# A newly searched order of steps, PSUM banks and engines in a fused attention and FFN kernel

## The chip, the cores and the metric

The kernel runs on one core of a Trainium2 chip. The metric is the device time of one execution in microseconds. The core has five engines with a queue of instructions each: TensorE (PE in the profile, its weight loads PEld), VectorE (DVE), ScalarE (ACT), GpSimd (POOL) and SyncE (SP). GpSimd and SyncE do hardly any arithmetic here: they issue the DMA transfers, ScalarE a few.

## What is computed

Linear attention with exponential features, and behind it a feed-forward network (FFN) with a squared ReLU. B is 8, H 8, S 576, D 64, the features 128, the model width 512, the FFN width 2048.

```
def phi(x):
    proj = np.einsum('bhsd,df->bhsf', x, w_phi)
    proj = proj - np.max(np.abs(proj), axis=-1, keepdims=True)
    return np.concatenate([np.exp(proj), np.exp(-proj)], axis=-1)
q_p, k_p = (phi(q), phi(k))
kv = np.einsum('bhsf,bhsd->bhfd', k_p, v)
z = np.sum(k_p, axis=2)
num = np.einsum('bhsf,bhfd->bhsd', q_p, kv)
den = np.einsum('bhsf,bhf->bhs', q_p, z)[..., None] + 1e-06
...
h = np.maximum(x @ w_in, 0.0)
return (h * h @ w_out).astype(np.float32)
```

Between the two, the 8 batches of attention output are laid out as 4608 tokens of width 512.

## The kernel before, in words

**Steps.** The kernel first lists 1680 steps in a plan, each with its engine, what it reads and writes, and a number in the order of listing (`add`, `Plan`). A step is one instruction, or a short run of matmuls, or one DMA. Then `plan.arrange()` gives the steps in the order of the list `ORDER`, and the last loop issues them so. `pin` ties each instruction to the one before on its engine, so every engine works through its own steps strictly in the order in which `ORDER` names them; SyncE's and GpSimd's DMA issues are such steps too. Across engines only the data and the buffers bind. Four more lists belong to `ORDER`:

- `BASES` gives each of the 377 uses of PSUM its bank.
- `STATES` says, for steps that two engines can do (copies out of PSUM, the ReLU of the FFN, the cast of the first k), which one does.
- `GATES` names for each load of batches 2 to 7 one step that it waits for beside its data, so that it isn't issued early.
- `FILL` puts n matmuls of zeros on TensorE ahead of a step, into a bank that is free there (line 961). They compute nothing that is used.

**Attention** of a batch works in groups of heads: Pk and Pq (L347, L379, L491) project k and q by `w_phi` in matmuls on half of the array's rows (64), two beside one another; Mk and Mq (L386, L405, L498, L531) take the maxima on VectorE; Ekp, Ekn, Eqp, Eqn (L394, L411, L544, L584) the exponentials on ScalarE; V (L428) scales v; KVs and KV (L450 on 64 rows, L462) sum up kv; the copy of kv to SBUF is kvc. For the output NA (L599, L648) multiplies the positive features, SA (L610, L660) scales the sum in PSUM, NB adds the negative ones, rd and xo (L614 to L674) divide. For batches 0 and 1 k and q are turned by TensorE (Txk, Txq, L320, with copies Cxk, Cxq on VectorE or ScalarE), and batch 0's output too (Tx, Txh, copies Cx, Cxh, L631, L699). Fq (L569) makes q's features already turned. From batch 2 on, k and q are turned by DMA transposes that SyncE issues (Xxk, Xxq, L331), the output of batches 1 to 7 by Xx (L708), and the features of q in batches 3 to 7 by Xf (L548). Xf reads one of two buffers qf, so the exponentials for the next but one group wait until it has landed.

**FFN.** Nine chunks of 512 tokens: one for each batch, and one of the 64 last tokens of every batch. F1 (L788; for chunk 0 in smaller pieces f1a, f1b, f1, f1p at L813, L799, L827) multiplies by `w_in`, relu and sq (L765, L767, L774) follow on ScalarE and VectorE, F2 (L882, the last tile F2h at L846) by `w_out`; ot copies the result, st stores it. Attention of batch c + 1 and the FFN of chunk c are mixed in `ORDER`.

**The beginning, by number.** 0 and 1: the first part of k by ScalarE's queue, cast by kcast:7 and 8. 2: `w_phi` by SyncE, cast by wcast:3 and 4. 6 and 5: VectorE sets the zeros of the fillers and of the identity matrix; ident:11 on GpSimd (L913) makes the identity of it, which every Txk needs. 9, 10: the 64 last tokens of batch 0's k; 12, 13: the rest of its k; 14, 19: its q; 15 to 18: its v; 26: batch 1's k, 1 MB of f32 that lands as 512 KB of bf16; 22 to 25: `w_in`; 36 to 39: `w_out`. All these loads are issued by GpSimd. 40, 49, 58, 66, 74 turn the five groups of k of batch 0, 42, 51, 60, 68, 76 project them.

Of the kernel before, what the change touches and what calls it, by code (L numbers as in the profile page):

```python
# [108 lines left out]
def kernel(  # L109
# [869 lines left out]
    210, 342, 242, 346, 243, 205, 485, 336, 224, 236, 233, 347, 267, 276, 226, 268, 182, 352, 183, 227, 277, 364,  # L979
    337, 353, 269, 366, 192, 489, 193, 549, 235, 278, 373, 254, 338, 237, 238, 490, 255, 239, 247, 257, 258, 241,  # L980
    228, 248, 259, 240, 229, 249, 230, 260, 270, 374, 333, 285, 232, 231, 343, 271, 244, 261, 272, 286, 262, 495,
    273, 274, 263, 344, 499, 287, 264, 265, 503, 339, 266, 294, 251, 295, 507, 252, 275, 296, 279, 250, 508, 288,
    280, 513, 253, 551, 289, 281, 547, 349, 282, 283, 556, 290, 354, 350, 284, 375, 379, 553, 291, 256, 292, 517,
    377, 744, 381, 348, 293, 297, 345, 531, 367, 376, 382, 298, 535, 370, 378, 380, 369, 299, 521, 552, 351, 422,
    300, 548, 387, 423, 525, 390, 546, 539, 557, 526, 389, 301, 371, 543, 388, 554, 413, 544, 438, 550, 482, 439,
    414, 372, 486, 440, 563, 483, 429, 368, 487, 416, 430, 383, 747, 492, 384, 555, 431, 474, 484, 740, 564, 395,
    417, 385, 478, 500, 475, 386, 476, 504, 479, 501, 488, 391, 480, 505, 514, 392, 493, 302, 510, 494, 393, 506,
    496, 511, 527, 404, 405, 565, 502, 396, 532, 497, 394, 498, 522, 398, 515, 518, 406, 523, 516, 540, 491, 519,
    397, 545, 533, 419, 524, 754, 447, 420, 399, 541, 400, 559, 448, 401, 749, 407, 408, 582, 403, 402, 449, 741,
    409, 583, 536, 739, 424, 415, 432, 562, 584, 410, 433, 737, 528, 411, 512, 418, 561, 520, 412, 434, 421, 529,  # L990
# [12 lines left out]
    627, 648, 780, 776, 1128, 913, 649, 929, 797, 650, 917, 651, 775, 899, 796, 921, 811, 774, 798, 903, 787, 781,
    831, 659, 782, 799, 783, 925, 784, 785, 786, 660, 860, 926, 832, 661, 873, 861, 864, 946, 662, 833, 663, 878,
    788, 834, 868, 862, 865, 907, 869, 664, 870, 819, 879, 886, 822, 880, 896, 866, 821, 856, 897, 887, 823, 820,
    882, 857, 812, 800, 874, 1312, 883, 789, 908, 942, 858, 801, 900, 884, 927, 875, 1120, 891, 876, 904, 901, 941,
    888, 902, 948, 1119, 790, 905, 949, 791, 1122, 792, 802, 951, 892, 898, 950, 793, 803, 824, 906, 893, 914, 835,
    794, 804, 894, 805, 843, 915, 825, 922, 845, 826, 916, 813, 923, 827, 806, 814, 918, 844, 815, 919, 910, 816,
    817, 846, 1068, 847, 828, 911, 829, 986, 924, 964, 960, 967, 1050, 830, 836, 1072, 848, 965, 962, 1321, 909,
    1124, 1054, 818, 849, 920, 966, 1123, 961, 1058, 1129, 988, 837, 912, 944, 1076, 838, 977, 963, 1121, 987, 1080,  # L1010
    1132, 839, 1081, 1062, 940, 840, 841, 978, 989, 1104, 1063, 842, 956, 998, 952, 1001, 990, 1086, 953, 1090, 1000,
    957, 1094, 955, 1002, 979, 1108, 954, 999, 1098, 968, 959, 970, 850, 1051, 969, 851, 1137, 958, 1059, 980, 1099,
    1112, 1052, 1060, 971, 852, 1126, 1047, 853, 1130, 854, 1010, 1116, 1127, 1013, 855, 1134, 1055, 1048, 1011, 991,
    1125, 1117, 1065, 1003, 1136, 1049, 1015, 1012, 1061, 1077, 1056, 1073, 1014, 1057, 1078, 1066, 1022, 1074, 1053,
# [93 lines left out]
```

## Time and profile before

| what | value |
|---|---|
| median of 3 runs | 347.04 us (346.59 to 347.21) |
| the profiled execution's own time | 346.94 us |
| its span, from first to last instruction | 345.2 us |
| granted TensorE clock, mean | 1.000 |
| moved by DMA | 51.51 MB, mean 149 GB/s |

The profile is of one execution. Busy times of an engine are sums over its instructions; matmuls overlap, so their durations are longer than their spacing from start to start. "Idle before" names what ended an idle time. The chain that ended last is followed back from the last instruction. Rows of the timeline give start, duration, engine, line, operation and tiles, with a count where equal instructions in a row are merged. A few matmul records can be missing, so a count of 15 can stand for 16.

### The profile page before, as it was taken

How to read it: one execution, taken by the hardware profiler on the slowest of the kernel's cores; microseconds unless marked ns; L12 is line 12 of the kernel's file. 1: busy time of each engine (PE TensorE's matmuls, PEld its weight loads, DVE VectorE, ACT ScalarE, POOL GpSimd, SP SyncE). 2: the span in 40 equal slices, each digit the busy share in tenths (PEclk: the TensorE clock that was granted, in tenths of full speed). 3: DMA queues.
4: the chain of work that ended last, by engine and by line, in shares of the span. 5: the costliest groups of instructions: out<-in, count | busy, mean ns of one | idle time of the engine just before them, and what ended most of it. 6: DMA issues, size and time to landing. Idle time of an engine off the chain costs nothing.

```text
span 345.2 us, 8387 instructions
## 1 busy us (share of the span) xinstructions
PE 333.0 (96%) x3361; PEld 188.2 (55%) x3393; DVE 262.7 (76%) x477; ACT 228.5 (66%) x401; POOL 95.5 (28%) x143
## 2 busy tenths in 40 slices
PE   7899999999999999999999999989999999999995
PEld 6679866545554554545545655545555454444443
DVE  2999998999887898799888888967888735655230
ACT  4998897588897996677887888497476213241121
POOL 8662550971910570104604160430000000000000
PEclk9999999999999999999999999999999999999999
DMA  9999999999999999999999999999882831100206
GB/s 129 169 190 194 197 178 176 124 142 247 124 170 197 207 156 197 190 186 191 186 186 169 201 187 180 169 133 154 182 166 54 170 92 56 45 0 2 91 32 151
DMA packets 142935, 51.51 MB, mean 149 GB/s; under 512 B 111472, under 2 KB 138416, under 8 KB 142896
## 3 DMA queue, kind: packets, MB, share of 16 engines
q1 hardware_dynamic: 97488, 32.35, 49.8%
q0 software_dynamic: 44960, 18.23, 47.5%
q8 instruction: 26, 0.43, 0.5%
q10 hardware_dynamic: 448, 0.39, 0.4%
q14 instruction: 13, 0.11, 0.1%
HBM read 36.73 MB, written 9.44 MB: 134 GB/s over the span
## 4 chain that ended last, share of the span: by engine, by line
PE 83%; DMA 6%; DVE 4%; ACT 2%; POOL 2%; issue 1%; SPq 1%; POOLq 0%; DVEq 0%; ACTq 0%
PE psum L882 32%; PE psum L788 30%; PE psum L648 5%; PE psum L347 5%; PE psum L462 3%; DMA xv<-in_v_dram 2%; PE psum L827 2%; DMA qpn<-qf 2%; DMA xT<-xo 1%; DVE mq L498 1%; PE psum L799 1%; PE psum L813 1%; PE psum L846 1%; PE psum L569 1%; DVE va L428 1%
## 5 line engine op out<-in xcount | busy, mean ns | idle before, releaser
L882 PE MATMUL psum<-wout,h 128*128 128x512 bf16 x528 | 128.2, 379 | 2.1 <-issue 0.6
L788 PE MATMUL psum<-xT,win 128*128 128x512 bf16 x448 | 105.5, 379 | 1.9 <-ACT hr L765 1.1
L765 ACT ACTIVATE hr<-psum 128x512 bf16<-128x512 f32 x103 | 60.2, 603 | 57.0 <-PE psum L788 35.3
L882 PEld LDWEIGHTS <-h 128*128 128x128 bf16 x560 | 51.4, 98 | 56.3
L788 PEld LDWEIGHTS <-win 128*128 128x128 bf16 x512 | 46.9, 98 | 53.5 <-issue 1.6
L774 DVE TENSOR_TENSOR h<-hr 128x512 bf16<-128x512 bf16 x144 | 56.4, 417 | 10.1 <-ACT hr L765 9.4
L544 ACT ACTIVATE qf<-psum 128x1024 bf16<-128x1024 f32 (+1 forms) x50 | 45.5, 942 | 15.1 <-PE psum L347 10.1
L405 DVE TENSOR_REDUCE mk<-psum 128x8 f32<-128x1024 f32 (+1 forms) x38 | 42.3, 1121 | 6.9 <-ACT kn L411 2.0
L767 DVE TENSOR_SCALAR hr<-psum 128x512 bf16<-128x512 f32 x41 | 27.8, 686 | 17.9 <-PE psum L788 17.3
L411 ACT ACTIVATE kn<-psum 128x1024 bf16<-128x1024 f32 (+1 forms) x38 | 35.7, 947 | 6.4 <-PE psum L347 4.7
L411 ACT ACTIVATE kp<-psum 128x1024 bf16<-128x1024 f32 (+1 forms) x38 | 35.5, 950 | 4.5 <-PE psum L347 3.0
L660 DVE TENSOR_TENSOR psum<-psum,en 128x520 f32<-128x520 f32 (+1 forms) x39 | 27.0, 701 | 13.5 <-ACT en L514 7.4
L648 PEld LDWEIGHTS <-qpn 128*128 128x128 bf16 x624 | 27.5, 98 | 13.4 <-issue 0.6
L269 POOL DMA_DIRECT2D xq<-in_q_dram x24 | 17.3, 725 | 52.2 <-DVE mq L531 14.2
L648 PE MATMUL psum<-kv,qpn 128*128 128x65 bf16 x624 | 30.6, 193 | 0.0
L531 DVE TENSOR_REDUCE mq<-psum 128x8 f32<-128x1024 f32 (+1 forms) x25 | 27.8, 1111 | 2.8 <-ACT qf L544 1.7
L584 ACT ACTIVATE qpn<-psum 128x1024 bf16<-128x1024 f32 (+1 forms) x30 | 26.8, 955 | 2.2 <-PE psum L569 1.3
L674 DVE TENSOR_TENSOR xo<-psum,rden 128x512 bf16<-128x512 f32 (+1 forms) x39 | 26.5, 686 | 0.8
L249 POOL DMA_DIRECT2D xk<-in_k_dram x27 | 19.8, 738 | 21.9 <-ACT en L508 14.6
L195 ACT ACTIVATE ot<-psum 128x512 f32<-128x512 f32 x23 | 13.8, 600 | 16.2 <-PE psum L882 16.1
L249 POOL DMA_DIRECT2D xv<-in_v_dram x27 | 19.9, 747 | 15.7 <-PE psum L648 11.1
L428 DVE TENSOR_TENSOR va<-xv,va 128x1280 bf16<-128x1280 bf16 (+2 forms) x34 | 23.5, 714 | 0.1
(78 smaller groups left out, 349.4 us busy)
## 6 DMA issues: line engine op xcount, KB each, us to landing
out_dram<-ot SPq DMA_DIRECT2D x32, 256.0 KB, 2.9
xk<-in_k_dram POOLq DMA_DIRECT2D x25, 128.0 KB, 5.4
xq<-in_q_dram POOLq DMA_DIRECT2D x24, 128.0 KB, 5.1
xv<-in_v_dram POOLq DMA_DIRECT2D x24, 128.0 KB, 5.0
win<-in_moe_w_in_dram POOLq DMA_DIRECT2D x4, 512.0 KB, 8.8
wout<-in_moe_w_out_dram POOLq DMA_DIRECT2D x4, 512.0 KB, 12.9
xq<-in_q_dram POOLq DMA_DIRECT2D x4, 256.0 KB, 7.2
out_dram<-ot SPq DMA_DIRECT2D x6, 128.0 KB, 2.4
```

The lines of the kernel that those rows point to most:

```text
L249: pin(nc.gpsimd.dma_start(out=x[:, m0 + a * 512 : m0 + z * 512].rearrange("p (h x) -> p h x", x=4 * D), in_=src[b][2 * a : 2 * z, 0:512, : ...
L405: pin(nc.vector.tensor_reduce(out=mk_view(g), in_=ps2(pj)[:, :, : n * Fd].rearrange("p e (i f) -> p e i f", f=Fd), axis=AX.X, op=ALU.max, ...
L411: pin(nc.scalar.activation(out=dst[slot][:, :, :n, :].rearrange("p e i f -> p e (i f)"), in_=ps2(pj)[:, :, : n * Fd], func=ACT.Exp, scale= ...
L531: pin(nc.vector.tensor_reduce(out=mqb[:, c, :, :n], in_=ps2(pj)[:, :, : n * Fd].rearrange("p e (i f) -> p e i f", f=Fd), axis=AX.X, op=ALU ...
L544: pin(nc.scalar.activation(out=o, in_=i_, func=ACT.Exp, scale=sgn))
L648: pin(nc.tensor.matmul(out=o[:, u // 4, u % 4 * D1 : (u % 4 + 1) * D1], lhsT=qpn[slot][:, sg * half + u * m : sg * half + u * m + P], rhs= ...
L660: pin(nc.vector.tensor_tensor(out=o, in0=o, in1=enb[:m, c, :].rearrange("t (b h) -> t b h", b=2).to_broadcast([m, 2, 4, D1]), op=ALU.mult))
L765: pin(nc.scalar.activation(out=hr[sl], in_=ps1(g), func=ACT.Relu))
L767: pin(nc.vector.tensor_scalar(out=hr[sl], in0=ps1(g), scalar1=0.0, scalar2=None, op0=ALU.max))
L774: pin(nc.vector.tensor_tensor(out=dst, in0=i_, in1=i_, op=ALU.mult))
L788: pin(nc.tensor.matmul(out=o, lhsT=win[mc // 4][:, kc, mc % 4 * P : (mc % 4 + 1) * P], rhs=x, start=(kc == 0), stop=(kc == KC - 1)))
L882: pin(nc.tensor.matmul(out=ps1(g), lhsT=h2[c % 2][mc // 4][:, mc % 4, tt * P : (tt + 1) * P], rhs=wout[mc // 4][:, mc % 4, :], start=(mc = ...
```

## The change

The plan, the steps and the code that issues them stay. The five lists are replaced: `ORDER` is another order of the same 1680 numbers, with the DMA issues at other places in it as well; `BASES`, `STATES` (82 steps instead of 80 on their other engine) and `GATES` are others; `FILL` has 117 matmuls before 12 steps instead of 119 before 11. On VectorE step 5 (the zeros of the identity) comes behind kcast:7 and wcast:3, and kcast:7 and 8 are VectorE's instead of ScalarE's. On GpSimd the first steps are 13, 9, 19, 11, 12, 14, 10, 26, 18, 17, 15 where they were 13, 12, 11, 14, 10, 9, 19, 18, 17, 16, 15, 26. The chunk 0 FFN starts with f1a:311 instead of f1a:307.

The diff, cut to the first lines of `ORDER`, the stretches in which the steps 464, 1181 and 1229 stand, and `FILL`:

```
 ORDER = [
-    2, 0, 1, 13, 12, 7, 8, 6, 5, 11, 3, 14, 10, 40, 41, 9, 4, 42, 19, 46, 74, 66, 44, 18, 43, 58, 45, 17, 75, 67, 47,
-    76, 16, 59, 68, 79, 48, 15, 71, 90, 77, 26, 88, 60, 21, 70, 91, 89, 28, 78, 49, 69, 27, 50, 20, 94, 80, 61, 81,
-    51, 72, 73, 92, 30, 95, 93, 98, 57, 22, 62, 52, 99, 31, 64, 54, 55, 23, 85, 53, 56, 84, 131, 24, 63, 82, 156, 25,
-    132, 157, 101, 37, 65, 133, 212, 83, 29, 128, 86, 102, 109, 87, 32, 110, 213, 111, 103, 129, 194, 214, 130, 104,
-    113, 215, 105, 112, 195, 96, 106, 100, 97, 365, 188, 107, 108, 218, 36, 217, 189, 114, 219, 121, 134, 34, 115,
-    216, 122, 116, 206, 33, 135, 123, 200, 207, 124, 38, 159, 117, 125, 201, 118, 136, 126, 160, 190, 137, 127, 119,
-    191, 142, 120, 161, 138, 145, 143, 220, 146, 307, 139, 308, 360, 147, 140, 221, 311, 312, 309, 162, 158, 141,
-    303, 144, 313, 163, 148, 223, 304, 149, 164, 322, 305, 165, 310, 166, 150, 323, 319, 151, 306, 234, 222, 152,
-    315, 314, 316, 320, 196, 325, 198, 321, 317, 197, 167, 153, 326, 328, 168, 154, 199, 318, 155, 169, 170, 174,
-    329, 324, 208, 356, 171, 186, 175, 331, 35, 209, 187, 176, 39, 245, 332, 184, 246, 177, 361, 172, 185, 334, 173,
-    359, 211, 178, 202, 357, 340, 203, 335, 355, 179, 477, 330, 358, 204, 180, 327, 481, 181, 363, 341, 225, 362,
...
-    745, 569, 708, 460, 428, 573, 712, 455, 587, 586, 461, 616, 462, 468, 463, 619, 690, 509, 469, 464, 609, 618,
-    578, 470, 716, 471, 580, 620, 472, 694, 617, 717, 581, 698, 628, 579, 736, 640, 631, 695, 756, 699, 665, 629,
...
-    1161, 1253, 1162, 1168, 1290, 1250, 1194, 1214, 1153, 1328, 1238, 1041, 1239, 1242, 1042, 1251, 1264, 1243, 1181,
-    1169, 1244, 1043, 1246, 1252, 1044, 1254, 1260, 1247, 1240, 1045, 1216, 1268, 1317, 1170, 1255, 1046, 1295, 1215,
-    1323, 1269, 1248, 1322, 1299, 1261, 1265, 1326, 1163, 1270, 1201, 1330, 1319, 1202, 1256, 1332, 1164, 1331, 1204,
...
-    1229, 1198, 1490, 1222, 1210, 1223, 1494, 1199, 1291, 1211, 1498, 1224, 1346, 1499, 1368, 1380, 1371, 1200, 1458,
-    1381, 1468, 1370, 1446, 1347, 1212, 1472, 1382, 1369, 1476, 1383, 1480, 1353, 1350, 1384, 1352, 1462, 1481, 1349,
...
-    40: (0, 26), 42: (0, 12), 76: (3, 11), 90: (1, 11), 49: (5, 2), 94: (5, 10), 98: (3, 4), 131: (7, 28),
-    212: (7, 6), 214: (7, 6), 116: (7, 3),
+    2, 0, 1, 13, 9, 19, 6, 7, 3, 5, 11, 8, 12, 4, 40, 14, 41, 42, 47, 10, 48, 74, 66, 75, 26, 44, 67, 76, 43, 45, 18,
+    68, 71, 77, 17, 58, 15, 46, 94, 69, 79, 27, 21, 59, 81, 70, 95, 49, 16, 60, 50, 78, 61, 51, 28, 90, 20, 73, 55,
+    88, 91, 72, 53, 30, 89, 92, 56, 57, 63, 98, 93, 24, 52, 54, 99, 156, 65, 34, 62, 206, 212, 22, 157, 131, 207,
+    101, 23, 64, 132, 218, 213, 25, 128, 82, 133, 31, 83, 102, 29, 129, 104, 105, 80, 103, 32, 106, 84, 194, 35, 85,
+    214, 100, 219, 86, 109, 110, 361, 87, 108, 215, 195, 111, 130, 33, 107, 200, 112, 96, 114, 36, 113, 201, 216,
+    115, 121, 134, 37, 122, 188, 116, 135, 97, 123, 217, 38, 190, 124, 117, 136, 125, 137, 39, 158, 118, 189, 142,
+    138, 159, 191, 143, 145, 160, 366, 126, 119, 127, 146, 220, 120, 139, 311, 140, 161, 312, 141, 221, 303, 144,
+    313, 148, 304, 147, 149, 307, 305, 308, 222, 150, 196, 151, 322, 152, 309, 233, 306, 199, 162, 310, 319, 163,
+    323, 197, 223, 164, 315, 165, 316, 166, 320, 153, 314, 317, 170, 154, 167, 171, 198, 186, 325, 187, 168, 155,
+    173, 169, 324, 208, 326, 174, 318, 331, 321, 175, 327, 172, 176, 209, 328, 332, 177, 329, 245, 178, 184, 210,
+    340, 185, 330, 179, 211, 546, 334, 180, 181, 356, 341, 202, 246, 337, 205, 357, 477, 342, 335, 203, 358, 338,
...
+    569, 558, 686, 572, 567, 461, 455, 616, 462, 712, 463, 619, 571, 464, 468, 690, 618, 469, 694, 573, 620, 617,
+    470, 716, 471, 472, 578, 717, 628, 579, 698, 586, 473, 609, 928, 630, 665, 588, 699, 755, 587, 669, 631, 666,
...
+    1152, 1160, 1149, 1299, 1159, 1150, 1118, 1161, 1250, 1181, 1254, 1215, 1242, 1162, 1251, 1041, 1238, 1182, 1042,
+    1216, 1252, 1260, 1239, 1243, 1043, 1246, 1318, 1044, 1244, 1045, 1133, 1261, 1303, 1240, 1169, 1247, 1134, 1201,
+    1248, 1330, 1322, 1264, 1332, 1262, 1202, 1168, 1320, 1333, 1268, 1325, 1331, 1204, 1256, 1269, 1307, 1218, 1203,
...
+    1486, 1351, 1228, 1337, 1195, 1490, 1196, 1226, 1440, 1302, 1207, 1219, 1208, 1197, 1444, 1229, 1220, 1209, 1198,
+    1445, 1494, 1210, 1211, 1327, 1221, 1498, 1212, 1222, 1199, 1468, 1223, 1499, 1200, 1230, 1368, 1380, 1346, 1383,
...
+    40: (0, 26), 42: (0, 11), 74: (3, 5), 76: (3, 7), 58: (4, 10), 49: (1, 24), 51: (5, 1), 88: (2, 4), 92: (2, 3),
+    156: (2, 6), 104: (5, 17), 121: (6, 3),
```

More of the change, by code (lines that the diff above doesn't have):

```diff
@@ L967 @@
 ORDER = [
[81 rows of a table removed]
[81 rows of a table added]
 ]
 BASES = (
[L1051 to L1054 removed]
+    '2014344022667555460560154672607205225563225457457070405242534266666056300064674474775442572340044070'
+    '5464242600246660633232227661207363176020027654260622044644756455643420345250220426732466426444401111'
+    '1002301311203026246413452664604002001133112370020710166224247652046500226664050652107151674773052075'
+    '37206240040034273250265436735646454673234753512671743126027144306542632647167'
 )
 STATES = (
[L1057 to L1059 removed]
+    '0000000000010000011111010110011000000000000100001000101110000100000010000111011001000100000001000111'
+    '0101011100100000001000000110000000011010010110100010001000101000011100000000011011000000101110101100'
+    '011001110100110110101000110011101'
 )
 GATES = {
[11 rows of a table removed]
[11 rows of a table added]
 }
 FILL = {
[L1075 to L1076 removed]
+    40: (0, 26), 42: (0, 11), 74: (3, 5), 76: (3, 7), 58: (4, 10), 49: (1, 24), 51: (5, 1), 88: (2, 4), 92: (2, 3),
+    156: (2, 6), 104: (5, 17), 121: (6, 3),
 }
```

7 lines of the change are left out of this document (removed), and 148 rows, old and new, of tables (GATES, ORDER).

## Prediction

> **What bounds the kernel now.** I read the page, then busy time by stretches, then who waited for whom on TensorE.
>
> ```profile
> span 345.2 us, 8387 instructions
> PE 333.0 (96%) x3361; PEld 188.2 (55%) x3393; DVE 262.7 (76%) x477; ACT 228.5 (66%) x401; POOL 95.5 (28%) x143
> PE 83%; DMA 6%; DVE 4%; ACT 2%; POOL 2%; issue 1%; SPq 1%; POOLq 0%; DVEq 0%; ACTq 0%
> ```
> ```profile
> 0.00:10.00 10.00, 7.55 (x106) 6.55 (x107) 3.64 (x11) 5.29 (x9) 8.89 (x17) 1.00 1.14 133
> 10.00:20.00 10.00, 8.29 (x122) 6.15 (x120) 10.00 (x16) 10.00 (x21) 5.44 (x9) 1.00 1.49 177
> 20.00:30.00 10.00, 9.76 (x198) 8.12 (x197) 9.24 (x21) 9.53 (x18) 6.25 (x9) 1.00 1.24 194
> ```
> ```profile
> PE psum L788 <- ACT hr L765: 1.1, 1, 1.1
> PE psum L788 <- DMA xT<-xo: 0.8, 1, 0.8
> ```
>
> TensorE is busy 96% of the span and carries 83% of the chain that ended last. The columns of the stretches are length, then PE, PEld, DVE, ACT, POOL busy, clock, DMA share, GB/s. In the second and third stretch VectorE (10.00, 9.24) and ScalarE (10.00, 9.53) are full while TensorE still has holes, which the filler matmuls partly paint over. So there are two regimes: a head that VectorE, ScalarE and the loads set, and a long body that TensorE sets. The chain shows where they meet:
>
> ```profile
> 8.11 8.09 DMA xv<-in_v_dram
> 28.46 0.55 PE psum L813 x8
> 337.98 3.51 PE psum L846 x32
> ```
>
> The first FFN matmuls start at 28.46, the last end at 341.49: 313.0 us in which TensorE waited for others only 1.1 + 0.8 us by the wait rows above. The rest is the same matmuls in any order, so a new order can win only these 1.9 us, the cost of changing between kinds of matmul, and some of the head.
>
> **The body: changes of array form.**
>
> ```profile
> 207.19 1.02 PE L882 MATMUL psum<-wout,h 128*128 128x512 bf16 x4
> 208.15 0.62 PE L347 MATMUL psum<-wphi,kT 64*128 64x128 bf16 x16
> 208.61 0.39 PE L347 MATMUL psum<-wphi,qT 64*128 64x128 bf16 x8
> 208.93 3.63 PE L882 MATMUL psum<-wout,h 128*128 128x512 bf16 x15
> 212.39 1.89 PE L788 MATMUL psum<-xT,win 128*128 128x512 bf16 x8
> 214.12 0.41 PE L648 MATMUL psum<-kv,qpn 128*128 128x65 bf16 x8
> ```
>
> Eight L788 matmuls take 214.12 - 212.39 = 1.73 us, 0.216 each, and an eight-fold L648 follows free of charge. Four L882 ought to take 0.86, but the 64-row L347 starts 0.96 later: 0.10 to go in. Sixteen L347 take 0.46, so eight take 0.23, and L882 starts 0.32 after them: 0.09 to come out. A visit to the 64-row form (Pk, Pq, Fq, KVs) costs about 0.2 us. Counting such visits in the two ORDER lists from the first f1a on gives 47 before and 45 after: **-0.4 us** (bounds 0 and -0.6, as the price differs by neighbour). Tx:139, four transposes of 0.056, now stands before the first f1a: **-0.2** of body.
>
> **The head.**
>
> ```profile
> 0.90 0.11 DVE L238 MEMSET ident<- 128x64 uint32 x1
> 2.90 0.32 POOL L913 TENSOR_SCALAR_AFFINE_SELECT ident<-ident 128x128 bf16<-128x128 bf16 x1
> 4.27 0.81 ACT L195 ACTIVATE xk<-ot 128x256 bf16<-128x256 f32 x2 [1.33 <-DMA ot<-in_k_dram]
> 4.44 0.31 DVE L230 CAST wphi<-wphi_f 64x128 bf16<-64x128 f32 x1 [3.43 <-DMA wphi_f<-in_w_phi_dram]
> 4.74 0.68 PE L320 MATMUL psum<-ident,xk 128*128 128x128 bf16 x4 [0.79 <-ACT xk L195]
> ```
>
> Now step 5, the memset of ident at 0.90, stands on VectorE behind kcast:7 and wcast:3, which wait for loads until 4.27 and 4.44. So it runs near 4.8, and POOL's ident:11, at 2.90 before, near 5.0. POOL issues in order: ident:11 comes after three loads (13, 9, 19), which end near 3.7, and **xk:12, xq:14, xks:10, xk:26 and all of V stand behind it**, some 1.3 us of POOL standing still. Txk:40 starts near 5.4 instead of 4.74, so VectorE's stream starts about 0.35 later. The next price is VectorE's work up to Cxh:120, which releases the first f1a:
>
> ```profile
> 5.46 0.42 DVE L193 COPY kT<-psum 128x512 bf16<-128x512 bf16 x1 [0.71 <-PE psum L320]
> 7.35 0.69 DVE L386 TENSOR_REDUCE mk<-psum 128x4 f32<-128x512 f32 x1 [1.10 <-ACT kp L394]
> 23.50 0.42 DVE L193 COPY qT<-psum 128x512 bf16<-128x512 bf16 x1
> 23.83 0.41 DVE L193 COPY kT<-psum 128x512 bf16<-128x512 bf16 x1
> 27.13 0.28 DVE L631 COPY xT<-psum 128x256 bf16<-128x256 bf16 x1
> 27.32 0.68 DVE L674 TENSOR_TENSOR xo<-psum,rden 128x512 bf16<-128x512 f32 x1
> 27.92 1.21 DVE L498 TENSOR_REDUCE mq<-psum 128x8 f32<-128x1024 f32 x1
> ```
>
> From 5.46 to 27.41 is 21.95 us, of which 1.9 wait (1.10 at 7.35). Put ahead of Cxh:120 are four copies (Cxq:95, 93, Cxk:50, 201) of 23.83 - 23.50 = 0.33, xo:138 (0.60) and Mq:143 (1.21): 3.13. Gone from there are three copies (Cxq:189, 191, Cxk:219), kvc:108 and a wcast (0.35 each): 1.69. Net +1.44. The wait at 7.35 goes, as Mk:48 now stands ahead of the exponentials of its bank; new waits come at Cxk:50 (xks:10 is late) and at V. With waits of 0.7 to 1.9, Cxh:120 ends at 5.8 + 20.05 + 1.44 + (0.7 to 1.9) = 28.0 to 29.2 and f1a starts 0.2 later. Before, f1a was held until 28.46 by other TensorE work. I take 28.9: **+0.45** (bounds -0.2 and +0.95).
>
> Loads could make it worse:
>
> ```profile
> xk<-in_k_dram POOLq DMA_DIRECT2D x1, 512.0 KB, 10.0
> 18.89 0.40 PE L320 MATMUL psum<-ident,xk 128*128 128x128 bf16 x4 [0.46 <-DMA xk<-in_k_dram]
> ```
>
> xk:26 landed at about 18.8, 2.6 after V at 16.20: the loads of this queue land in order of issue. Now it is issued ahead of V, with two small loads more, so V lands near 18 and 19.5. VectorE reaches the first V near 17.4 (2.2 us of other work was put ahead), so about 0.6 of this shows, and is in the waits above. The Trainium skill, "DMA: Bandwidth & Descriptors", section "Anatomy of one DMA", fits a transfer of this path at 2.0 us plus its bytes at 436 GB/s; by that 512 KB lands in 3.2 us, no load would bind, and the head would be an estimated 0.7 us better. The row's 10.0 speaks against it for a full queue.
>
> ```profile
> 26.16 3.87 ACT L584 ACTIVATE qpn<-psum 128x1024 bf16<-128x1024 f32 x4
> ```
>
> ScalarE: these four exponentials (Eqp:160 to Eqn:147) now stand behind Cxq:189 and 191 and start about 1.2 later, with a relu between them, ending near 32.1; NB:150 would run at 31.8. **+0.3** (bounds 0 and +1).
>
> **The body's waits.** SP issues in order, and a transpose blocks it for long.
>
> ```profile
> 98.05 3.32 SPq L331 DMA_TRANSPOSE kT<-xk  x1
> 106.14 4.40 DMA xT<-xo
> 214.12 2.77 SPq L331
> 216.94 7.26 DMA qpn<-qf
> 224.28 1.02 ACT L544 ACTIVATE qf<-psum 128x1024 bf16<-128x1024 f32 x1 [2.27 <-DMA qpn<-qf]
> DMA to landing us min/median/max: 3.1/5.2/8.6
> ```
>
> The 0.8 wait: Xx:464 issued at 106.14, late behind Xxk:755 (3.32) and others, and landed after 4.40, with three F2 groups (2.6) and 1.3 of small work standing between it and its first F1. After, four F2 groups (3.45) and 1.15 stand there, and Xxk:755 comes behind it: **-0.8** (bounds 0 and -0.9). The 1.1 wait: Xf:1181, behind Xxk:1328 (2.77), took 7.26; ScalarE stood 2.27 at Eqn:1204, with the relu that TensorE wanted behind it. Both transposes keep their order, and the TensorE work between Xf:1181 and Eqn:1204 grows only from 6.6 to 7.1: **0** (bounds -1.1 and +0.5). New risk: between Xf:1229 and Eqn:1383 stand 3.8 us (6.1 before, to its first user then), and before Xf:823's first user 5.9 (8.5), against landings of 3.1 to 8.6: **+0.2** (bounds 0 and +2). PSUM banks and the 82 instead of 80 steps on their other engine cost nothing by themselves: VectorE is 76% busy over the span. The tail keeps its last 32 F2h matmuls and stores. Fillers are 117 instead of 119, in holes.
>
> **Sum:** -0.4 - 0.2 + 0.45 + 0.3 - 0.8 + 0 + 0.2 = -0.45 us. The profiled execution took 346.94 (span 345.2 and 1.7 around it), 0.1 under the median 347.04. So 346.5 in the profiled run's terms and **346.6** beside the median.
>
> **Rivals.**
> 1. *No waits:* both old waits vanish, none forms, NB:150 isn't held. -0.4 - 0.2 + 0.45 - 1.9 = -2.05: 345.0. For: most distances from Xx to F1 are longer. Against: the Xf pattern at 1181 is unchanged. 0.12.
> 2. *Waits form elsewhere* behind transposes: at Eqn:1383 1.1 and at one F1 0.8 instead of 0.2: +1.25, 348.3. For: landings up to 8.6 against 3.8 and 5.9. Against: later on ScalarE has slack. 0.17.
> 3. *Slower by the head:* POOL's pause behind ident:11 leaves the load queue dry, and V lands 1.3 us later than I reckon, near 19.4; the first V on VectorE then waits 2 us instead of 0.6. It decides once V's first half lands after about 18. Price +1.4 to +1.6: +1.05, 348.1. For: V's landing is on the chain (8.09). Against: three loads are queued before the pause. 0.22.
> 4. *The head isn't bound by loads:* VectorE then waits only 0.7, f1a starts at 28.2, -0.25 instead of +0.45: -1.15, 345.9. For: 2.2 us of other work stand ahead of V. Against: the 10.0 us of the load ahead of V. 0.04. The Trainium skill's fit, named above, would come to this.
> 5. *The lists change nothing that matters:* the engines keep to ORDER, but every shift is absorbed: 347.0. 0.03.
>
> **Numbers.** The forecast, 345.6 to 347.2, has 0.42, of it 0.24 below 346.35 and 0.18 above. A measurement of this kernel tells about 0.2% (0.7 us) from no change. Faster: 0.24 + 0.12 + 0.04 = 0.40. Same: 0.18 + 0.03 = 0.21. Slower: 0.17 + 0.22 = 0.39. The range takes in rivals 2 to 5 and the upper half of rival 1: 344.9 to 348.9.
>
> **What would show it.** The ident memset near 4.8 and the affine select near 5.0 on POOL; the first L813 matmul at 28.6 to 29.2 (over 30: rival 3); no TensorE wait for xT near 110; a ScalarE wait for qpn<-qf near 223 followed by a TensorE wait for hr. Between the first L813 and the last L846 I expect 312.1 us; under 311 is rival 1, over 313.5 rival 2. If ident's memset runs before 2 us, or V holds VectorE for none or over 1.5 us, the head is wrong; if waits of TensorE above 0.5 us appear at other places than these, the body is.

## The result, and the profile after

| | kernel before | changed kernel |
|---|---|---|
| median of 4 executions | 346.81 us (346.58 to 347.21) | 353.39 us (351.32 to 357.63) |
| the profiled execution's own time | 346.94 us | 357.63 us |
| its mean granted TensorE clock | 1.000 | 0.985 |
| first L813 (start of the body) | 28.46 us | 29.23 us |
| last L846 (end of the body) | 341.49 us | 352.17 us |

The changed kernel is slower: ratio 1.0159 (95% interval 1.0119 to 1.0200). I had put the range at 344.9 to 348.9 us and slower by over 0.2% at 0.39; the time lies 4.5 us above the range. All ratios here leave out executions more than 1.5% above their kernel's fastest, which also hits some whose own waits are merely longer, so medians over all executions stand beside them.

The page of the changed kernel, the lines that answer to those of the kernel before, with the row of the granted clock, which was all nines there:

```profile
span 355.9 us, 8414 instructions
PE 337.5 (95%) x3361; PEld 190.0 (53%) x3391; DVE 266.5 (75%) x485; ACT 224.5 (63%) x393; POOL 95.6 (27%) x143
PEclk9998999999999999989989999999999999999999
PE 80%; DMA 8%; DVE 4%; ACT 4%; issue 2%; POOL 1%; SPq 0%; DVEq 0%; ACTq 0%
```

DMA has 8% of the chain instead of 6%, and in three slices the clock falls to eight tenths. Who waited for whom, TensorE's rows (us in total, times, longest):

```profile
PE psum L788 <- ACT qf L544: 4.0, 1, 4.0
...
PE psum L347 <- DVE xo L674: 2.7, 1, 2.7
...
PE psum L882 <- DVE ot L193: 0.8, 1, 0.8
...
PE psum L462 <- DVE va L428: 0.4, 1, 0.4
```

Both old waits (0.8 for xT, 1.1 for hr) are gone and two long new ones have come; with two small ones they are 7.9 us in the body instead of 1.9. The chain, from three windows of it, shows what stands behind each:

```profile
29.23 2.26 PE psum L813 x24
```
```profile
144.88 10.04 DMA qpn<-qf
...
155.00 0.16 ACT qf L544
...
157.10 4.44 PE psum L788 x12
```
```profile
175.31 7.72 DMA xT<-xo
...
183.12 0.70 DVE xo L674
...
183.87 0.40 PE psum L347 x8
184.26 2.71 PE psum L882 x7
```

Near 157: the transpose Xf:799, issued at 144.88, takes 10.04 us. ScalarE stands at Eqp:821, which overwrites the buffer qf that Xf:799 reads; behind it, in ScalarE's order, is the exponential that frees the bank of the next F1. Near 184: Xx:806, issued at 175.31, takes 7.72 us. VectorE stands at xo:841, which overwrites the xo that Xx:806 reads, and a Pk waits for its banks. In both a transpose gives a buffer back late, and an engine that works in order carries the wait to TensorE.

Look also at the matmuls right after: twelve L788 take 4.44 us, 0.37 each instead of 0.216. The table by stretches (length, then busy time of PE, PEld, DVE, ACT, POOL, then the clock) shows why:

```profile
24.20:27.62 3.42, 2.48 (x28) 1.34 (x29) 2.43 (x8) 2.47 (x5) 1.45 (x2) 1.00 1.24 206
27.62:31.03 3.41, 3.31 (x35) 2.94 (x34) 2.42 (x6) 2.40 (x5) 0.91 (x2) 0.50 1.44 195
...
153.90:157.32 3.42, 0.22 (x2) 0.10 (x2) 1.03 (x2) 2.32 (x6) 0.00 (x0) 1.00 1.08 148
157.32:160.73 3.41, 3.41 (x10) 1.17 (x9) 0.90 (x2) 2.21 (x4) 0.00 (x0) 0.50 1.29 270
...
181.20:184.63 3.43, 0.77 (x10) 0.43 (x10) 1.51 (x3) 1.10 (x2) 0.00 (x0) 1.00 1.31 59
184.63:188.04 3.41, 3.19 (x8) 1.21 (x8) 3.41 (x4) 2.86 (x4) 0.00 (x0) 0.50 0.79 143
```

Three times a stretch in which TensorE had stood idle for a part (it was busy 2.48, 0.22 and 0.77 us of some 3.42) is followed by 3.41 us at clock 0.50, which cost 1.7 us each. With that the account of the profiled execution, the longest of the four, closes: the body starts 0.8 later, has 6.0 us more of waits, and loses 1.8 + 3.4 + 3.4 us at half clock, which is 4.3 us; that makes 11.1, the measured difference is 10.7, and the remaining -0.4 is the body's own work. Set apart: 311.2 us of body without waits before, 310.8 after. The new order costs nothing where nothing waits; it loses by late transposes and by the half clock behind them.

### The profile page after: what moved, and what is told of

Same layout as the page of the kernel before. It is cut to its first block, busy times and chain, and to the rows that moved or that the text cites. A ratio compares the mean times of both kernels' runs of the same rounds, so it can differ in the third digit from the quotient of the medians.

```text
span 355.9 us, 8414 instructions
## 1 busy us (share of the span) xinstructions
PE 337.5 (95%) x3361; PEld 190.0 (53%) x3391; DVE 266.5 (75%) x485; ACT 224.5 (63%) x393; POOL 95.6 (27%) x143
## 4 chain that ended last, share of the span: by engine, by line
PE 80%; DMA 8%; DVE 4%; ACT 4%; issue 2%; POOL 1%; SPq 0%; DVEq 0%; ACTq 0%
PE psum L882 32%; PE psum L788 27%; PE psum L648 5%; PE psum L347 5%; PE psum L462 4%; DMA qpn<-qf 3%; DMA xT<-xo 2%; PE psum L827 2%; DMA xv<-in_v_dram 2%; PE psum L813 1%; ACT qpn L584 1%; PE psum L799 1%; DVE mq L498 1%; PE psum L846 1%; DVE mk L405 1%
## 5 line engine op out<-in xcount | busy, mean ns | idle before, releaser
L882 PE MATMUL psum<-wout,h 128*128 128x512 bf16 x530 | 129.4, 382 | 2.9 <-issue 0.9
L788 PE MATMUL psum<-xT,win 128*128 128x512 bf16 x448 | 107.4, 383 | 4.0 <-ACT qf L544 4.0
L765 ACT ACTIVATE hr<-psum 128x512 bf16<-128x512 f32 x96 | 56.2, 599 | 56.2 <-PE psum L788 28.4
L882 PEld LDWEIGHTS <-h 128*128 128x128 bf16 x560 | 51.7, 98 | 57.9 <-issue 3.4
L788 PEld LDWEIGHTS <-win 128*128 128x128 bf16 x512 | 47.4, 98 | 56.3 <-issue 6.5
L405 DVE TENSOR_REDUCE mk<-psum 128x8 f32<-128x1024 f32 (+1 forms) x38 | 42.3, 1119 | 3.8 <-PE psum L347 2.5
L767 DVE TENSOR_SCALAR hr<-psum 128x512 bf16<-128x512 f32 x48 | 32.7, 686 | 11.4 <-PE psum L788 9.4
L249 POOL DMA_DIRECT2D xk<-in_k_dram x27 | 19.7, 733 | 68.7 <-PE psum L788 11.6
L195 ACT ACTIVATE ot<-psum 128x512 f32<-128x512 f32 x19 | 11.3, 597 | 33.2 <-PE psum L882 33.2
L193 DVE COPY ot<-psum 128x512 f32<-128x512 f32 x16 | 11.0, 688 | 26.4 <-PE psum L882 25.7
L531 DVE TENSOR_REDUCE mq<-psum 128x8 f32<-128x1024 f32 (+1 forms) x25 | 27.6, 1109 | 1.7 <-PE psum L347 1.1
## 6 DMA issues: line engine op xcount, KB each, us to landing
wout<-in_moe_w_out_dram POOLq DMA_DIRECT2D x4, 512.0 KB, 11.1
```

The costliest lines, as they stand in the source:

```text
L249: pin(nc.gpsimd.dma_start(out=x[:, m0 + a * 512 : m0 + z * 512].rearrange("p (h x) -> p h x", x=4 * D), in_=src[b][2 * a : 2 * z, 0:512, : ...
L405: pin(nc.vector.tensor_reduce(out=mk_view(g), in_=ps2(pj)[:, :, : n * Fd].rearrange("p e (i f) -> p e i f", f=Fd), axis=AX.X, op=ALU.max, ...
L531: pin(nc.vector.tensor_reduce(out=mqb[:, c, :, :n], in_=ps2(pj)[:, :, : n * Fd].rearrange("p e (i f) -> p e i f", f=Fd), axis=AX.X, op=ALU ...
L765: pin(nc.scalar.activation(out=hr[sl], in_=ps1(g), func=ACT.Relu))
L767: pin(nc.vector.tensor_scalar(out=hr[sl], in0=ps1(g), scalar1=0.0, scalar2=None, op0=ALU.max))
L788: pin(nc.tensor.matmul(out=o, lhsT=win[mc // 4][:, kc, mc % 4 * P : (mc % 4 + 1) * P], rhs=x, start=(kc == 0), stop=(kc == KC - 1)))
```

## The experiments

**Theory A:** the loads of the next batches share the DMA engines with the transposes; the new lists put a burst of fourteen loads (129 to 143 us) beside them, so these land late. **Theory B:** the new order of the three compute engines leaves the transposes too little room, whatever the queues do. **Theory C:** SyncE's new order issues them too late. In what part loads and transposes would hinder one another (the engines, the memory) no run here separates.

**1. The changed kernel again**

> The changed kernel once more, unaltered, to see which of its losses come back. The profile shown has two long waits of TensorE (4.0 us behind ScalarE's wait for qpn<-qf near 157, 2.7 us behind VectorE's wait for xT<-xo near 184), and three stretches of 3.41 us at half clock, each of which costs 1.71 us. If the waits belong to the order, both are in this profile again, over 2 us each, and the times lie in steps of about 1.7 us between 350 and 358. If they are chance of one execution, they are gone or elsewhere, and the times are near 350.

Median 354.05 us over 6 executions (350.04 to 358.30), ratio 1.0119 [1.0075, 1.0163]. Its profile is of an execution of 351.53 us without half clock:

```profile
ACT qf L544 <- DMA qpn<-qf: 9.8, 3, 4.4
...
DVE xo L674 <- DMA xT<-xo: 2.0, 1, 2.0
...
PE psum L788 <- ACT qf L544: 1.8, 1, 1.8
...
PE psum L347 <- DVE xo L674: 1.6, 1, 1.6
...
PE psum L882 <- ACT hr L765: 1.5, 1, 1.5
```

The same two waits at the same steps, but shorter than the 2 us each that were expected, a third of 1.5 behind Xf:823 (the user that the prediction gave 5.9 us of room) and smaller ones, 7.3 us in all; so their places belong to the order, and their length to the execution. Less what their mean clocks (0.984 to 1.000) say was lost, the times lie between 348.7 and 352.6. The first L813 is at 27.72 here: the body started 0.7 us earlier than in the kernel before, which contradicts the prediction's head.

**2. The loads later.** Nine loads of the burst are moved behind Mq:832 and wait for it.

```
-    933: 454, 934: 467, 935: 653, 936: 589, 937: 872, 938: 474, 939: 592,
+    933: 454, 934: 832, 935: 832, 936: 832, 937: 832, 938: 832, 939: 832,
...
-    943: 619,
+    943: 832,
...
-    1126: 881, 1129: 417,
+    1126: 832, 1129: 832,
```

> Nine of the fourteen loads that GpSimd issues between 129 and 143 us are held until Mq:832 (about 150). Theory that the loads crowd out the transposes: Xx:627 to Xf:799 land after 4 to 6.5 us instead of 8.7 to 10.0, ScalarE waits under 1 us for qpn<-qf at Eqp:821, the 4.0 us wait of TensorE near 157 falls under 0.8, and the half-clock stretch behind it goes too: 4 to 5.5 us off a run that has both. Rival, that the transposes are slow since SyncE issues them in a bunch: their landings stay over 8 us and the wait stays over 3 us. The wait near 184 stays in both.

Median 358.20 us (355.71 to 364.28), ratio 1.0295 [1.0253, 1.0337]: 4 us worse. But Xf:811 and Xf:799 now landed after 4.4 and 5.3 us, and the wait near 157 is gone, as theory A said. What came instead shows in SyncE's issues:

```profile
148.03 0.90 SPq L900 DMA_DIRECT2D out_dram<-ot  x1
159.79 4.52 SPq L331 DMA_TRANSPOSE qT<-xq  x1
164.41 1.79 SPq L548 DMA_TRANSPOSE qpn<-qf  x1
```

SyncE stood from 149 to 159.8 at Xxq:947, which needs the loads that I held back, and Xf:823, ready at 150.2, stood behind it; TensorE waited 10.0 us in one piece near 170. A wait moved from one in-order queue into another is not removed.

**3. Xx:806 first.** SyncE's steps, taken out of `ORDER`:

```
-    835, 909, 847, 818, 806, 830,
+    835, 806, 909, 847, 818, 830,
```

> In SyncE's order Xx:806 stands right behind Xf:835, as in the kernel before, and no longer behind st:909, Xf:847 and Xx:818. Theory that SyncE's order makes the second wait: Xx:806 is issued 3.4 us earlier (near 171.9 instead of 175.3), lands near 179, VectorE no longer waits for it at xo:841, the 2.7 us wait of TensorE near 184 falls under 0.5, and its half-clock stretch goes: 2.5 to 4.4 us. Rival, that the loads between 172.7 and 178 make it land late: it still lands after 182 and at least 2 us of the wait stay. The wait near 157 stays in both.

```profile
166.16 4.06 SPq L548 DMA_TRANSPOSE qpn<-qf  x1
170.31 1.22 SPq L708 DMA_TRANSPOSE xT<-xo  x1
```

Issued at 170.31 instead of 175.31, Xx:806 landed after 3.8 us instead of 7.72; xo:841 ran at 178.23 without waiting, and the wait near 184 is gone from the profile (the one near 157 was 3.9 there). Median 351.56 us over 12 executions (347.36 to 353.69), ratio 1.0078 [1.0035, 1.0121]: 2.5 us below the 354.05 of the unaltered kernel in the same rounds, though the intervals of the two ratios overlap. So at this place theory C holds: SyncE's order put the transpose where it was late. Theory A has a share in it: in the unaltered kernel Xx:806 stood among nine loads issued from 172.72 to 178.06, here it went ahead of them all.

**4. Fillers in the two waits**

```
-    156: (2, 6), 104: (5, 17), 121: (6, 3),
+    156: (2, 6), 104: (5, 17), 121: (6, 3), 882: (1, 50), 952: (6, 32),
```

> 50 filler matmuls (2.8 us) are put before the F1 that waits near 157 and 32 (1.8 us) before the Pk that waits near 184; nothing else. Theory that the half clock is the price of an idle TensorE and comes on top of the wait: where the two waits are long, the F1 and the Pk start at the same time as without fillers, but no half-clock stretch follows them, so a run that had both is 3.4 us shorter, and the mean clock is 0.995 or more in every run. Rival, that the clock falls for another reason: half-clock stretches remain behind both places and the times stay as in the unaltered kernel.

```profile
152.92 2.95 PE L961 MATMUL psum<-warm 128*128 128x128 bf16 x50 [0.25 <-DVE hr L767]
156.28 1.89 PE L788 MATMUL psum<-xT,win 128*128 128x512 bf16 x8 [0.41 <-ACT qf L544]
```

The F1 still waits for ScalarE, 0.41 us past the fillers, but its eight matmuls take 1.89 us, full speed, and the clock was 0.998 to 1.000 in five of six executions (0.993 in one), against 0.984 to 0.990 in four of six unaltered. So the half clock is the price of a TensorE that stands idle in the wait. Keeping the clock up bought nothing: median 353.76 us (351.36 to 356.53), ratio 1.0186 [1.0136, 1.0236], probably since fillers of 2.95 and 1.95 us push TensorE back where the waits are shorter (1.8 and 1.6 us in the second profile).

**5. Both places mended.** The loads wait for Mq:820 with q's six first, and SyncE's steps are:

```
-    946, 891, 947, 823, 927, 873, 664, 835, 909, 847, 818, 806, 830,
+    946, 891, 823, 927, 873, 664, 947, 835, 806, 909, 847, 818, 830,
```

> The changed kernel with both places mended, and without the wait that holding the loads had made: the nine loads are held until Mq:820 (near 146) with q's six first, Xxq:947 stands behind Xx:664 in SyncE's order so that it waits for them with nothing urgent behind it, and Xx:806 stands right behind Xf:835. Theory (the waits come from where the loads and transposes stand in the two DMA queues, the rest of the new order costs nothing): TensorE's waits over 0.35 us, 7.3 us in the second profile of the unaltered kernel, fall to 3 or less, no half-clock stretch, first L813 near 27.9, time 344.0 to 347.0, at or below the kernel before. Rival (the new order itself lacks room, and the wait moves on to the next transpose): waits of 4 us or more in sum, some of them at Xf:823, Xf:835 or a Pq of batch 5, and a time of 348 to 352.

Median 353.78 us (351.14 to 357.91), ratio 1.0239 [1.0162, 1.0316]: the rival. The old places were quiet; the nine loads now ran with sixteen others between 146 and 172, Xxq:947 took 11.6 us and Xf:835 10.8, and a Pq of batch 5 waited:

```profile
PE psum L347 <- DMA qT<-xq: 3.5, 2, 3.4
```

**6. A burst of loads in the kernel before.** Nine loads that it issues between 155 and 172 come at 132 to 138:

```
-    1119: 635, 1120: 834, 1121: 1050, 1122: 589, 1129: 879,
+    1119: 637, 1120: 637, 1121: 637, 1122: 637, 1129: 637,
...
-    940: 662, 941: 729, 942: 717, 944: 453,
+    940: 637, 941: 637, 942: 637, 944: 637,
```

> The kernel before with one thing altered: nine loads that it issues between 154 and 185 us and that nobody needs before 176 (942, 1120, 941, 1119, 1122, 1121, 1129, 940, 944) are issued in a row from 131 on, as the changed kernel has fourteen there; SyncE's and all other orders stay. Theory that the loads crowd out the transposes: Xx:639 to Xf:799, which landed after 5.0 to 7.1 us, now take 8 to 10, ScalarE waits 1.5 to 3 us for qpn<-qf at Eqp:833 or Eqp:821, TensorE waits 1 to 3 us behind it near 150, and the kernel is 1 to 4 us slower than before. Rival (the place of the steps, not the loads): landings stay at 5 to 7 us, no new wait over 0.5, time within 0.7 us of before.

```profile
137.26 6.66 SPq L331 DMA_TRANSPOSE qT<-xq  x1
143.98 2.99 SPq L708 DMA_TRANSPOSE xT<-xo  x2
147.50 6.01 SPq L548 DMA_TRANSPOSE qpn<-qf  x2
```
```profile
PE psum L788 <- DMA xT<-xo: 5.4, 2, 4.6
```

Median 353.86 us (353.15 to 354.80), ratio 1.0203 [1.0162, 1.0244]: a tuned order made as slow as the changed one by moving nine loads that nobody needs before 176. Theory A holds; I had the place wrong. The burst hit Xxq:947 (11.2 us to landing, 5.4 before; 6.66 us for its issue alone, 3.5 before), everything behind it in SyncE's queue came 5 us late, and an F1 waited 4.6 us for xT near 151, with a half-clock stretch behind it. Some 0.9 us of this execution's loss are not the burst's: another half-clock stretch, at 19.0, long before the moved loads, put its first L813 at 29.31.

**7. The head: xk:12 second on GpSimd.** GpSimd's steps:

```
-    13, 9, 19, 11, 12, 14, 10, 26,
+    13, 12, 9, 19, 11, 14, 10, 26,
```

> The changed kernel with GpSimd's load xk:12 moved from behind ident:11 to second place, as in the kernel before; nothing else. Theory that the head's gain comes from the light loads beside the first k: with two heavy loads issued first the first cast of k waits until 3.8 to 4.5 instead of 2.9, Txk:40 starts 0.5 to 1 later than 4.34, and the first L813 comes at 28.4 or later instead of 27.6 to 28.0. Rival (VectorE makes the casts instead of ScalarE, and the loads have no say): the cast starts before 3.2 and the first L813 stays under 28.1. My prediction's theory, that GpSimd standing still behind ident:11 costs, would make this kernel faster in the head, as xk:12 no longer stands behind it.

```profile
2.93 0.29 DVE L193 CAST xk<-ot 128x256 bf16<-128x256 f32 x1 [1.99 <-DMA ot<-in_k_dram]
```
```profile
4.41 0.33 POOL L913 TENSOR_SCALAR_AFFINE_SELECT ident<-ident 128x128 bf16<-128x128 bf16 x1
```

The first cast starts at 2.93 as in the unaltered kernel, so the loads beside it have no say: that theory falls. The first L813 comes at 28.89 all the same, a us later. ident:11 now stands behind four issues on GpSimd instead of three and starts at 4.41, against 3.94 and 3.96 in the two profiles of the unaltered kernel; but one execution doesn't show that this made the us. With the unaltered first steps ident:11 started at 4.26 in two profiles (experiments 2 and 8), and the first L813 came at 29.14 in one and at 27.66 in the other. The prediction's theory, that xk:12 behind ident:11 costs, finds no support: with xk:12 ahead of it the head was no faster. One execution, 357.19 us; most of that is waits further down, the largest a Pk's 4.0 for kT near 90, where the two profiles of the unaltered kernel have none (the kernel with fillers has 1.6 there): which transpose comes late changes between executions.

**8 to 10. Undoing the queues.** The loads of batches 2 to 7 in the order and with the gates of the kernel before; SyncE's first 98 DMAs in its order; both.

```
-    928: 717, 929: 449, 930: 610, 931: 583,
+    928: 397, 929: 684, 930: 478, 931: 677,
...
```

> The changed kernel, but the 107 loads of batches 2 to 7 that GATES names stand on GpSimd in the order and behind the gates of the kernel before; all other orders are the changed kernel's. If the loads' places alone make the waits: the waits of TensorE over 0.35 us fall from 7 to under 3 us in sum, the transposes Xx:627 to Xf:799 land after 4 to 7 us, time 344.5 to 348. If SyncE's order makes them: they stay at 5 us or more, time 350 or more. The waits can also come out at other places, since the gates now open at other times; then both are needed, and the next kernel decides.

> The changed kernel, but SyncE's first 98 DMAs stand in the order of the kernel before; loads and all other orders are the changed kernel's. If the loads' places alone make the waits, they stay: landings of 8 to 10 us between 130 and 145, 5 us or more of waits, time 350 or more; Xx:806 lands in time for xo:841, as in the kernel that mended this place alone (about 2 us better than unaltered there). If SyncE's order makes them: under 3 us of waits, time 344.5 to 348.

> The changed kernel with the loads of batches 2 to 7 and SyncE's first 98 DMAs both in the order (and gates) of the kernel before. What is left of the change is the order of TensorE, VectorE and ScalarE, the banks, the engines, the fillers and the head. If the two DMA queues are the whole loss: body waits of 2 us or less, first L813 at 27.6 to 28.0, time 344.3 to 346.3, at or under the kernel before, by the head's 0.6 us. If the new order of the three engines lacks room for the transposes wherever they stand: 5 us or more of waits and 349 or more.

| | median | range | ratio | waits in the body |
|---|---|---|---|---|
| loads as before | 365.61 us | 363.55 to 370.55 | 1.0514 [1.0469, 1.0560] | 16.5 us |
| SyncE as before | 367.32 us | 363.98 to 373.67 | 1.0547 [1.0488, 1.0606] | 18.1 us |
| both as before | 357.21 us | 355.56 to 359.21 | 1.0295 [1.0253, 1.0337] | 9.5 us |

None of the three did what theories A and C promised; with both queues as before these rows of TensorE are left:

```profile
PE psum L788 <- DMA xT<-xo: 2.6, 2, 2.1
PE psum L648 <- DMA qpn<-qf: 2.5, 2, 2.1
...
PE psum L347 <- DMA qT<-xq: 2.0, 1, 2.0
PE psum L788 <- ACT qf L544: 1.7, 1, 1.7
...
PE psum L788 <- ACT hr L765: 1.1, 1, 1.1
```

So the order of the compute engines and the two queues seem to be one plan: with the new compute order the old queue orders, one or both, do worse than the new ones. That speaks for theory B as far as it goes, but not against A: the crowds may only meet other transposes.

**11 and 12. No loads after batch 1.** Two lines in the last loop, in both kernels, leave out the loads that `GATES` names (108 of them; the expectations say 107):

```
         now[0] = op
+        if op.seq in GATES:
+            continue
         op.fn()
```

> The changed kernel with the 107 loads of batches 2 to 7 left out: these batches compute on the q, k and v of batches 0 and 1. Every other instruction, SyncE's transposes and stores too, stays in its order. Theory A, that the transposes land late since loads share the DMA engines with them: landings between 130 and 185 fall to 2.4 to 5 us, waits of TensorE over 0.35 us in the body to under 1.5 us in sum, no half-clock stretch, time 343.5 to 346. Theory B, that the new order of TensorE, VectorE and ScalarE leaves the transposes too little room whatever the loads do (both queues put back as before still left 9.5 us of waits): 4 us or more of waits stay, time 348 or more.

> The kernel before with the same 107 loads left out. Its waits were 0.8 and 1.1 us. Theory A: both go, time 344.5 to 346, so that the changed kernel without loads is 0 to 1.5 us the faster of the two, by its head. Theory B: it stays at 345 to 347 and is 3 us or more faster than the changed kernel without loads.

The landing of Xf from issue (min, median, max) in the changed kernel, then without loads, then in the kernel before without loads:

```profile
DMA to landing us min/median/max: 3.2/5.2/10.0
```
```profile
DMA to landing us min/median/max: 3.1/4.4/5.8
```
```profile
DMA to landing us min/median/max: 3.1/4.4/6.1
```

The longest landing of Xf falls from 10.0 to 5.8, the median of Xx (xT<-xo and xS<-xo) from 4.4 to 2.5, and from 37 us on neither kernel has a wait of TensorE over 0.35 us. Theory A is shown in that the waits need the loads, and B as a cause by itself is refuted: with uncrowded transposes the new order has room enough, and the bodies take 312.4 us (changed) and 312.1 (before), waits for `win` at their start included. The whole times, 346.99 us (344.81 to 348.24; ratio 0.9994 [0.9970, 1.0017]) and 352.47 (351.29 to 353.96; 1.0158 [1.0127, 1.0189]), are over what theory A promised and don't compare: without loads nothing holds back batch 2's transposes, which start at 12.84 us, and TensorE then waits in its head for q, 2.3 us in the changed kernel and 5.6 in the kernel before.

**13 to 15. Thinning the crowd.** Batch 5's q (934 to 939) is loaded behind xk:928, near 111, where GpSimd waits anyway, and Xx:806 stands first; then also 943, 1129 and 1126 behind xk:1119; then, without these three, four more of SyncE's DMAs moved.

```
-    928: 717, 934: 467, 935: 653, 936: 589, 937: 872, 938: 474, 939: 592,
+    928: 717, 934: 717, 935: 717, 936: 717, 937: 717, 938: 717, 939: 717,
```
```
-    718, 615, 644, 682, 736, 656, 627, 639, 651, 811, 799, 946, 891, 947, 823, 927, 873, 664, 835,
+    718, 682, 736, 615, 644, 656, 627, 639, 651, 811, 799, 946, 664, 891, 823, 947, 927, 873, 835,
```

> The changed kernel with the six loads of batch 5's q (934 to 939) issued right behind xk:928, near 111 to 115, where GpSimd stands waiting, instead of between 130 and 143; and Xx:806 right behind Xf:835 as in the kernel that mended that place. Theory A: with eight loads instead of fourteen beside them Xx:627 to Xf:799 land after 5 to 7 us, the wait near 157 falls under 1.5 us, time 347 to 350, some 2 us under the kernel with Xx:806 alone. Theory B: the wait stays at 2 us or more, or comes out at Xf:608 to Xf:644 between 100 and 125, time 351 or more.

> The same as the kernel with batch 5's q early, and three more loads (943, 1129, 1126) taken out of the burst to stand behind xk:1119 near 151, so that five are left in it. Theory A: the wait near 157 goes (under 0.5 us), time 346 to 349. Theory B: as for the kernel with q early, 351 or more.

> The kernel with batch 5's q early and Xx:806 mended, and four more of SyncE's DMAs moved within its order: the stores 682 and 736, ready near 100 and issued near 130, come right behind st:718 (near 125), which ends ScalarE's 3.9 us wait for out_dram<-ot that held TensorE 2.6 us near 137; Xx:664, ready at 146 and issued at 158.5, right behind Xxk:946; Xxq:947 behind Xf:823. Theory A (with the crowd thinned, each wait left has one DMA that stands too late behind others): no wait of TensorE over 0.8 us in the body, time 344.5 to 348, level with the kernel before or better. Rival: the waits move on to other DMAs of the two queues, 2 us or more in sum, time 349 or more.

With q early the profiled execution has the shortest span of all profiles of the new order with its loads, 345.9 (347.62 us). Xf:799 lands after 5.5 us, both old places are quiet, and one wait over 0.5 us is left in the body:

```profile
ACT ot L195 <- DMA out_dram<-ot: 3.9, 1, 3.9
...
PE psum L882 <- ACT ot L195: 2.6, 1, 2.6
```

ScalarE waited, near 136, for a store of ot that SyncE had issued at 129.8, 31 us after it was ready. But the median over 10 executions is 354.29 us (347.62 to 358.35; ratio 1.0073 [1.0027, 1.0118]; the kernel before in the same rounds: 347.12, 346.10 to 353.76). With three loads more moved: 354.42 (352.45 to 358.12; 1.0192 [1.0159, 1.0224]); in its profile Xf:823 takes 10.03 us, and TensorE waits 3.4 behind it near 167. With the stores mended: 354.84 over 12 (348.41 to 361.16; 1.0067 [1.0030, 1.0104]), and a new place:

```profile
128.55 13.98 DMA qpn<-qf
...
142.57 0.62 PE psum L648 x8
```

Beside the q loads issued at 109.6 to 112.9 and four more at 118.5 to 120.5 Xxk:755 takes 8.9 us, Xf:632 8.1 and Xxq:756 11.8 (5.5, 4.3 and 8.3 in the first profile of the unaltered kernel), SyncE falls behind, and Xf:644, ready at 116.7, is issued at 128.55 and takes 13.98. The rival: the wait moves on. No version with its loads beats the kernel before.

**16. The kernel before again**

> The kernel before once more, unaltered, for a second profile. If the late first load of the profile that the prediction used (the first cast of k at 4.27 us, against 2.8 to 2.95 in every profile since) was chance, the cast starts before 3.1 and Txk:40 before 4.0. The first L813 then tells what the head of the changed kernel (27.6 to 28.0 in most profiles) gains: 27.5 to 28.0 here means nothing, 28.4 or later means 0.5 us or more. The waits at the places of the two long waits of the changed kernel stay under 0.5 us each.

```profile
2.94 0.91 ACT L195 ACTIVATE xk<-ot 128x256 bf16<-128x256 f32 x2
```
```profile
28.67 0.55 PE psum L813 x8
```

347.41 us. The late first load of the first profile was chance, yet the first L813 is where it was. Its two waits are back at the same places (0.9 us for xT near 111, 1.3 for hr near 227), and Xf:799 landed after 4.8 us.

## Why the prediction was wrong, step by step

- **The sum's term for new waits, "+0.2 (bounds 0 and +2)", is the step that failed**; it measured +6.0 us of waits and +4.3 us of half clock in the profiled execution, 5.4 and 0 in the second. The waits come from transposes that land late beside the loads of later batches. I compared the TensorE work ahead of each user with "landings of 3.1 to 8.6", which are those of the kernel before, under its loads. `GATES` and GpSimd's order changed with the rest, and of that I worked out the head only. With the kernel before's landing of 5.16 us Xf:799 would have been there at 150.0, before ScalarE came to Eqp:821 at 150.3; it took 10.04. The room did shrink, from 6.4 us between the issue of Xf:799 and ScalarE's arrival at Eqp:821 in the kernel before to 5.4; but the no-loads kernels show that without long landings it is enough, and the burst in the kernel before shows what a crowd of loads costs.
- **The places I named** were not where it was lost: Eqn:1383 waited for its transpose in neither of the first two profiles (Xf:1229 landed after 3.85 us in both), Xf:823 held TensorE 1.5 us in the second. Near 157 I had no term, though the room of Xf:799 was there to be worked out. Near 184 the wait came from a swap in SyncE's list that I had in the diff and didn't follow: three DMAs more ahead of Xx:806.
- **The half clock is not in the prediction at all.** A wait that leaves TensorE idle for most of such a stretch of 3.41 us costs 1.7 us on top; fillers in the wait kept the clock up.
- **Rival 2 named the mechanism** (waits behind transposes) and priced it 1.25 us; "later on ScalarE has slack" doesn't help where ScalarE itself stands at the buffer.
- **The old waits.** That for xT near 110 went, as I said (Xx:464 landed 3.0 us after its issue). That for hr near 226, which I let stay at 0, went too: Xf:1181 landed after 4.58 us instead of 7.26, behind Xxk:1328 in both kernels, with one store more between them; why it was quicker I didn't test.
- **The head, "+0.45", has the wrong sign in most profiles:** the first L813 at 27.56 to 27.95 in nine of twelve profiles with this head, in the timeline's starts, and 29.0 to 29.1 in three (two of them with a half-clock stretch from 27.6 or 27.8 on), against 28.39 and 28.60 in two profiles of the kernel before and 29.31, behind a half-clock stretch, with the same head in experiment 6. ident's memset ran at 3.75, not near 4.8: I took the cast's start at 4.27 from one execution, and every later profile has 2.82 to 3.01. The first V ran at 17.49 without waiting. What makes the new head 0.7 us faster in the nine stays open; experiment 7, one execution, doesn't settle whether the loads' first places have a part in it.
- **NB:150, "+0.3":** no wait of TensorE there; 0.
- **Visits and Tx:139, "-0.6":** the body without waits and half clock is 310.8 to 311.3 us after and 311.2 in both profiles before: between -0.4 and +0.1, mostly not there.

So the forecast was made of small terms that mostly came near zero, and the one that turned out large was sized from a trace in which its cause had not yet changed.

## What to carry to other kernels

A transfer's time from issue to landing depends on what runs beside it (Xf took 3.1 to 5.8 us in the changed kernel without the later loads, and up to 14.0 in a version with them); when a change moves transfers, the old landings may not be used to judge room, neither for the moved ones nor for those they now meet. Where engines work in order, find every instruction that overwrites a buffer which a DMA still reads: these are where a late landing turns into a wait of the busiest engine. And put a price on the clock: the waits of 2.7 and 4.0 us cost 1.7 us more each here.

## What the runs showed of the hardware

The granted clock changed on a fixed grid: in the trace's record of the first profile it fell at 27.62, 157.32 and 184.63 us and returned 3.41 us later each time, and the distances, 129.70 and 27.31, are 38 and 8 times 3.413. The Trainium skill, "TensorE: Matmul & The Clock Gate", section "Part 1: The HAM clock gate (the "warmup" mystery)", tells of a free-running window of about 3.4 us after which an idle TensorE drops to half rate; the trace agrees in window and rate. It need not be idle: 0.77 us of 3.43 busy was enough, and in the head 2.48 of 3.42, made of small matmuls and transposes, while a window with about half its time busy with L882 and L347 (177.1 to 180.5 in the second profile, a wait of 1.6 us) kept the full clock. Over all 18 profiles, cut along this grid, each of the 14 full-clock windows with less than 1.3 us of TensorE busy was followed by half clock; from 1.36 to 1.44 two were and one was not; from 1.50 on, in the body, none was. Three windows with 2.4 to 2.5 us busy, all in the head, were too, and others like them were not, so busy time alone doesn't decide. What the gate counts no run here shows.

That a crowded transpose also blocks the engine that issues it was larger than I had reckoned with: the issue of Xxq:947 alone grew from 3.5 to 6.66 us with the burst beside it.
